# Six of seven Strassen products of a dense layer with channels on partitions: results turned in 32x32 squares

## The chip, the core and the metric

The kernel runs on one core of a Trainium2 chip. The metric is the device time of one execution in microseconds (us), lower is better; the time shown for a kernel is the median of its runs. The core's engines are named as in the profile: PE (TensorE, matrix products; PEld are its weight loads), DVE (VectorE), ACT (ScalarE), POOL (GpSimd) and SP (SyncE). SP, ACT and POOL each also issue DMA transfers, and each runs its own instructions in the order in which they were written.

## What is computed

A transformer block on 2048 tokens with 512 channels, float32. The second half is what matters here: a dense layer to 1792 channels, the Mish activation, and a dense layer back to 512, scaled by `gb` and added to the residual.

```python
x = x + ga * _A_ref(h, A_wqkv, A_wo)             # linear attention
h = _layernorm(x, axis=-1) * (1 + cb) + sb
h = jnp.einsum("bsd,df->bsf", h, w1) + b1        # 512 -> 1792
act = h * jnp.tanh(softplus(h))                  # Mish
x = x + gb * jnp.einsum("bsf,fd->bsd", act, w2)  # 1792 -> 512
```

## The kernel before, in words

Tokens come in four blocks of 512 (b = 0 to 3), channels in tiles of 128, so the hidden layer has 14 tiles (f), taken as 7 pairs (g). Every float32 product is made of three matmuls on upper and lower parts of its operands (`mm3`: upper x upper, upper x lower, lower x upper; its second argument is the stationary operand, the third the moving one). `split` makes these parts: the upper on ACT (line 84), the lower on DVE (line 90).

Blocks 2 and 3 are handled together with a seven-product (Strassen) scheme, for both dense layers. This change is about the second layer of these two blocks, after the helper `two_pairs`/`pair_unit` has made the hidden layer. Its operands are cut in two ways each: tokens in block 2 and block 3, hidden tiles in the even and the odd one of a pair, output channels in a left and a right half of 256. The seven products `m1` to `m7` each run over the 7 pairs. `seventh` makes one product's share of one pair, called a unit here: before, for each of four groups of 128 tokens, an `mm3` with the activations (128 x 128) stationary and the weights (128 x 256) moving, so 12 matmuls of 256 columns; a PSUM bank then holds two groups of 128 tokens by 256 channels. `m1` and `m2` (`e_unit`) are made in the gaps between the products of the first layer (`gap`, called by `pair_unit`); the units of the last pair, and `m4`, `m6`, `m7`, `m5` follow in a loop over `units`, and `m3` ends the kernel, token group by token group. The inner loop of `m3` is no part of this change.

The left operands are sums of the activations of both blocks (`left_sums`, line 1353, DVE) which are then split; in the closing loop `ahead_of` lists these splits, taken from five units ahead on. The weights of a unit come by a DMA that POOL issues (`load_wt`). The residual rows of blocks 2 and 3 (`x1d`, written by `o_post` to DRAM) are loaded by SP (`load_r`) into tiles `rq[n, c, i]`: block, half of the channels, half of the rows or channels. When a product is complete, `finish` adds its two banks where they belong: straight to the residual tiles (`add_r`) or to the running sum `U`, and SP stores finished tiles (`store`). After `m3`, four adds (line 1477) and four stores end the kernel.

The order on each engine is the order of writing, shaped by generators: `spawn` adds one, each `tick()` advances every running generator by a step, and `spawn_idle` adds background work of which `width[0]` (here 3) generators advance per tick. All SBUF tiles `sb(...)` share 101 slots; PSUM has 4 banks under the tag `acc`, 3 under `h` and 1 under `tp`. For blocks that the first layer reads with channels on partitions, `load_squares` loads DRAM rows in 32 x 32 squares (four transfers of 32 partitions for a tile), and `dve.transpose` turns each square in place (line 262).

Of the kernel before, what the change touches and what calls it, by code (L numbers as in the profile page):

```python
# [27 lines left out]
def block_kernel(ctx: ExitStack, tc: tile.TileContext, x, wqkv, wo, w1, b1t, w2, c, wmodt, out):  # L28
    nc = tc.nc
    act, dve, pool, pe, sp = nc.scalar, nc.vector, nc.gpsimd, nc.tensor, nc.sync  # L30
# [4 lines left out]
    drp = ctx.enter_context(tc.tile_pool(name="drp", bufs=1, space=bass.MemoryType.DRAM))  # L35
# [16 lines left out]
    def spawn(gen):  # L52
        fresh.append(iter(gen))

    def spawn_idle(gen):

        idle_work.append(gen)

    def tick():

        running.extend(fresh)
        fresh.clear()
        for g in list(running):
# [10 lines left out]
    def mm3(o, st, mv, start, stop):  # L74

        pe.matmul(o, st[0], mv[0], start=start, stop=False)  # L76
        pe.matmul(o, st[0], mv[1], start=False, stop=False)  # L77
        pe.matmul(o, st[1], mv[0], start=False, stop=stop)  # L78
# [163 lines left out]
    nd, yd = {}, {}  # L242

    def to_dram(key, b, t, v):
        if (key, b) not in nd:
            nd[key, b] = drp.tile([512, D], F32, name=f"{key}d_{b}")
        pool.dma_start(nd[key, b][P * t:P * (t + 1), :], v)

    def load_squares(key, b, order=(0, 2, 1, 3)):


        for j in order:
            y = yd[key, b, j] = sb(f"y_{key}_{b}_{j}")
            for c in range(4):
                lo = P * j + 32 * c
                sp.dma_start(y[32 * c:32 * (c + 1), :].rearrange("q (m r) -> q m r", r=32),
                             nd[key, b][:, lo:lo + 32].rearrange("(m q) r -> q m r", q=32))

    def turn(key, b, j, keep, name, sc0, sh0):

# [299 lines left out]
    for k in range(4):  # L560
        hi, lo = sb(f"hT_x_0_{k}h", F32R), sb(f"hT_x_0_{k}l", F32R)
# [265 lines left out]
    for b in range(1, NB):  # L827
        last = b == NB - 1
# [86 lines left out]
    x1d = {}  # L915

    def o_post(p, b, t):
        r = xt["r", b, t]
        dve.tensor_tensor(r, p, r, op=ALU.add)  # L919
        if b >= 2:  # L920
            yield
            if t % 2 == 0:
                x1d[b, t // 2] = drp.tile([P, 2, D], F32, name=f"x1d_{b}_{t // 2}")
            pool.dma_start(x1d[b, t // 2][:, t % 2, :], r)  # L924

    def o_unit(b, t, tag="acc"):
        p = ps(tag, f"o_{b}_{t}")
# [150 lines left out]
    for b in range(1, NB):  # L1078
        for t in range(4):
            n = 4 * b + t  # L1080
# [161 lines left out]
    G = NF // 2  # L1242
# [70 lines left out]
    L = NB - 2  # L1313
    pairs, EARLY = [5, 6, 0, 1, 2, 3, 4], 5
    banks, rq, U = {}, {}, {}
    width[0] = 3

    def load_r(n, c):

        for i in range(2):  # L1320
            rq[n, c, i] = sb(f"rq_{n}_{c}_{i}", F32, (P, 2, D // 2))
            sp.dma_start(rq[n, c, i], x1d[L + n, i][:, :, D // 2 * c:D // 2 * (c + 1)])

    def store(n, c, i, lo=0, hi=2):
        r0 = 512 * (L + n) + 2 * P * i
        sp.dma_start(out[r0 + P * lo:r0 + P * hi, D // 2 * c:D // 2 * (c + 1)].rearrange("(t p) c -> p t c", p=P),
                     rq[n, c, i][:, lo:hi, :])

    def seventh(name, tag, left, right, n, last):

        if n == 0:
            banks[name] = [ps(tag, f"{name}_{i}") for i in range(2)]
        for t in range(4):
            h = t % 2
            mm3(banks[name][t // 2][:, D // 2 * h:D // 2 * (h + 1)], [a[:, P * t:P * (t + 1)] for a in left], right,
                n == 0 and h == 0, n == last and h == 1)

    def bank(name, i):
        return banks[name][i].rearrange("p (t c) -> p t c", t=2)
# [16 lines left out]
    left, sums_of = {}, {}  # L1356
# [9 lines left out]
    def add_r(n, c, i, v, op=ALU.add):  # L1366
        dve.tensor_tensor(rq[n, c, i], rq[n, c, i], v, op=op)

    def finish(name):
        for i in range(2):  # L1370
            p = bank(name, i)
            if name == "m2":
                U[i] = sb(f"U_{i}", F32, (P, 2, D // 2))
                act.activation(U[i], bank("m1", i), AF.Copy)
                add_r(0, 0, i, bank("m1", i))
                add_r(0, 0, i, p)
                store(0, 0, i)
            if name == "m4":
                add_r(1, 0, i, p, ALU.subtract)
            if name == "m6":  # L1380
                dve.tensor_tensor(U[i], U[i], p, op=ALU.add)
                add_r(0, 1, i, U[i])
            if name == "m7":
                dve.tensor_tensor(U[i], U[i], p, op=ALU.add)
                add_r(1, 0, i, U[i])
                store(1, 0, i)
                add_r(1, 1, i, U[i])
            if name == "m5":
                add_r(0, 1, i, p)
                add_r(1, 1, i, p)  # L1390
                store(1, 1, i)
            yield

    wt, SUM = {}, {"m5": 0, "m6": 1, "m7": 2, "m4": 3}
# [15 lines left out]
    for n, g in enumerate(pairs):  # L1410
        if n < 5:
            if n:
                load_rows(n)
            if n:
                load_wb(pairs[n + 1])
        if n == 5:
            load_wb(pairs[6])
            load_r(0, 0)
        if n == 6:
            for m in pairs[:5]:  # L1420
                load_wt("m4", m)
        def gap(c, m):
            def unit():
                e_unit(c, m)
            return unit

        if n in (3, 5):
            spawn_idle(w2_sums(SUMS_KEPT[n // 2 - 1]))
        if n == 0:
            spawn_idle(w2_sums(2))  # L1430
            begun = [pair_begin(L, pairs[i], ("tp" if i else "h", "acc")) for i in range(2)]
            tick()
        elif n == 1:
            two_pairs(L, pairs[0], g, begun, (gap(0, 0), gap(0, 1)))
            for i in range(2):
                spawn_idle(left_trail(pairs[i]))
        else:
            pair_unit(L, g, n % 2, (gap(1, 0), gap(1, 1)) if n == 2 else (gap(0, n - 1), gap(1, n - 1)))
            if n < EARLY:
                spawn_idle(left_trail(g))  # L1440

    names = ["m4", "m6", "m7", "m5", "m3"]
    units = [(name, n) for name in names for n in range(G)]
    ahead_of = units[EARLY:]
    loads = list(units)
    loads = loads[5:]
    load_r(1, 0)
    tags = {"m4": "h", "m6": "acc", "m7": "acc", "m5": "h"}
    for k, (name, n) in enumerate(units[:4 * G]):
        for _ in range(2 if k in (6, 10, 14, 18) else 1):  # L1450
            if ahead_of:
                nm, m = ahead_of.pop(0)
                spawn(left_prep(nm, pairs[m]))
        for _ in range(2 if k < 3 else 1):
            if loads:
                nm, m = loads.pop(0)
                load_wt(nm, pairs[m])
        if k in (3, 8):
            load_r(k // 8, 1)
        seventh(name, tags[name], left.pop((name, pairs[n])), wt.pop((name, pairs[n])), n, G - 1)  # L1460
        if n == G - 1:
            spawn(finish(name))
        tick()
        if k == 1:
            e_unit(0, G - 1)
            e_unit(1, G - 1)
            spawn(finish("m2"))
            tick()

    last = [ps("acc", f"m3_{t}") for t in range(4)]  # L1470
    for t in range(4):
        p = last[t][:, 0:D // 2]
        for n, g in enumerate(pairs):
            mm3(p, [a[:, P * t:P * (t + 1)] for a in left["m3", g]], wt["m3", g], n == 0, n == G - 1)
        tick()
        v = rq[0, 1, t // 2][:, t % 2, :]
        dve.tensor_tensor(v, v, p, op=ALU.add)
        store(0, 1, t // 2, t % 2, t % 2 + 1)


# [30 lines left out]
```

## Time and profile before

| | before |
|---|---|
| time, median of 3 runs | 488.17 us (488.06 to 488.59) |
| time of the profiled execution | 488.34 us |
| its span, first to last instruction | 486.6 us |
| granted PE clock over the span | 1.000 of full speed |
| PE busy, matmuls | 481.6 us (99%), 2594 of them |
| PEld busy | 406.5 us (84%) |
| DVE / ACT / POOL busy | 378.3 / 295.7 / 148.7 us |
| DMA | 100.66 MB in 91296 packets |

The profiled execution took 1.7 us more than its span; the rest lies around it. In the rows of the profile, an operation is named by its output and inputs, with buffer numbers left out, so that all of `m1` to `m7` are called `m`, and the split left operands `l_m`. Where rows are listed in time, the first two numbers are start and duration in us.

### The profile page before, as it was taken

To read this page: it belongs to the slowest core of one execution; us is meant where nothing else is said; L and a number is where in the kernel's file an instruction comes from. 1 tells how busy PE (TensorE), PEld (TensorE's weight loads), DVE (VectorE), ACT (ScalarE), POOL (GpSimd) and SP (SyncE) were. 2 spreads that over 40 slices of the span, in tenths; PEclk is the share of its full clock that TensorE was granted. 3 is DMA by queue.
4 is the path that set the end of the run, shared out by engine and by line. 5 is a ranking of instruction groups with operands and counts; after the bars stand their busy time and mean duration, and the time that the engine had idled before them with its cause. 6 is when DMAs were issued, how large, how long until landed. Compare 5 with 4: busy or idle time off the path is not lost.

```text
span 486.6 us, 7712 instructions
## 1 busy us (share of the span) xinstructions
PE 481.6 (99%) x2594; PEld 406.5 (84%) x2594; DVE 378.3 (78%) x731; ACT 295.7 (61%) x528; POOL 148.7 (31%) x248
## 2 busy tenths in 40 slices
PE   8999999999999999999999999999999999999997
PEld 6788887878878888888888888888888888899997
DVE  7989988999799699976867665899543666769772
ACT  6777686866546979647767665674165554568100
POOL 4583320000122124103422435225444410545200
PEclk9999999999999999999999999999999999999999
DMA  8805598244863417488799999979999813789412
GB/s 315 292 14 126 143 156 256 68 145 140 294 169 109 133 36 253 131 291 292 250 339 361 335 207 210 347 225 311 373 356 340 238 26 105 193 205 248 114 44 86
DMA packets 91296, 100.66 MB, mean 207 GB/s; under 512 B 32337, under 2 KB 56921, under 8 KB 91258
## 3 DMA queue, kind: packets, MB, share of 16 engines
q1 hardware_dynamic: 62088, 54.68, 35.9%
q0 software_dynamic: 29024, 45.24, 33.5%
q8 instruction: 20, 0.33, 0.3%
q10 hardware_dynamic: 146, 0.26, 0.1%
q14 instruction: 18, 0.15, 0.1%
HBM read 63.97 MB, written 34.08 MB: 201 GB/s over the span
## 4 chain that ended last, share of the span: by engine, by line
PE 93%; DVE 4%; ACT 1%; issue 1%; POOL 0%; ACTq 0%; DVEq 0%
PE p_a L1137 20%; PE p_s L1137 8%; PE oacc L77 5%; PE oacc L78 5%; PE oacc L76 5%; PE m L78 5%; PE m L77 5%; PE m L76 5%; PE o L76 3%; PE o L78 3%; PE o L77 3%; PE pq_a L404 3%; PE pk L78 2%; PE pk L76 2%; PE pk L77 2%; PE gacc L77 2%
## 5 line engine op out<-in xcount | busy, mean ns | idle before, releaser
L207 POOL TENSOR_TENSOR rs_n<-rs_n,half 128x1 f32<-128x1 f32 x16 | 11.4, 712 | 62.2 <-DVE rs_n L202 35.5
L1142 DVE TENSOR_TENSOR cb<-p_s,u 128x512 f32<-128x512 f32 x28 | 19.2, 687 | 13.1 <-ACT u L1178 13.1
L1172 ACT ACTIVATE u<-p_a 128x512 f32<-128x512 f32 x12 | 7.2, 598 | 28.0 <-PE p_a L1137 28.0
L1147 ACT ACTIVATE u<-p_a 128x512 f32<-128x512 f32 x14 | 8.4, 598 | 25.7 <-PE p_a L1137 17.4
L1129 ACT ACTIVATE ub<-cb,b1c 128x512 f32<-128x512 f32 x28 | 20.0, 717 | 4.9 <-DVE cb L1142 4.7
L1408 POOL DMA_DIRECT2D wt_m<-w2t x20 | 14.0, 703 | 27.1 <-DVE cb L1142 14.7
L1178 ACT ACTIVATE u<-p_a 128x512 f32<-128x512 f32 x14 | 8.4, 597 | 15.9 <-PE p_a L1137 15.9
L1142 DVE TENSOR_TENSOR c<-p_a,u 128x512 f32<-128x512 f32 x14 | 9.6, 688 | 9.1 <-PE p_a L1137 7.9
L895 POOL DMA_DIRECT2D rden_d<-rden x2 | 1.4, 720 | 46.3 <-DVE rden L893 46.3
L295 ACT ACTIVATE e_k<-pk 128x512 f32<-128x512 f32 x15 | 8.9, 592 | 10.8 <-PE pk L78 10.8
L774 POOL DMA_DIRECT2D w2b<-w2d x20 | 10.6, 542 | 14.4 <-DMA y_n<-nd 4.8
L768 POOL DMA_DIRECT2D wb<-w2d x14 | 9.9, 711 | 14.9 <-PE p_a L1137 12.4
L1106 ACT ACTIVATE u<-p_a,b1c 128x512 f32<-128x512 f32 x14 | 9.6, 686 | 6.7 <-PE p_a L1137 6.7
L298 DVE SCALAR_TENSOR_TENSOR ku<-e_k,relu_k 128x512 f32<-128x512 f32 x15 | 10.7, 712 | 3.1 <-ACT relu_k L296 3.1
L298 DVE SCALAR_TENSOR_TENSOR q<-e_q,relu_q 128x512 f32<-128x512 f32 x16 | 10.7, 684 | 2.9 <-ACT relu_q L296 2.9
L207 POOL TENSOR_TENSOR rs_x<-rs_x,half 128x1 f32<-128x1 f32 (+1 forms) x10 | 7.8, 782 | 15.8 <-DVE rs_x L202 14.6
L821 POOL DMA_DIRECT2D a1b<-rd_a x10 | 5.4, 542 | 22.4 <-PE p_a L1137 11.4
L307 POOL DMA_DIRECT2D ku<-ku x8 | 7.2, 898 | 16.5 <-DVE ku L298 16.5
L919 DVE TENSOR_TENSOR r<-o,r 128x512 f32<-128x512 f32 x16 | 10.8, 675 | 0.9 <-PE o L78 0.9
L907 DVE SCALAR_TENSOR_TENSOR q<-q,rd 128x512 f32<-128x512 f32 x16 | 10.5, 683 | 0.6 <-DMA rd<-rden_d 0.4
L924 POOL DMA_DIRECT2D x1d<-r x8 | 4.4, 549 | 20.9 <-DVE r L919 20.9
L183 DVE SCALAR_TENSOR_TENSOR wm<-wm,sc_row 128x512 f32<-128x512 f32 x16 | 10.5, 674 | 0.0
(1623 smaller groups left out, 1975.9 us busy)
## 6 DMA issues: line engine op xcount, KB each, us to landing
wm<-in_wmodt_dram SPq DMA_DIRECT2D x24, 256.0 KB, 5.3
w2b<-w2d POOLq DMA_DIRECT2D x20, 256.0 KB, 6.6
wt_m<-w2t POOLq DMA_DIRECT2D x20, 256.0 KB, 4.2
r<-in_x_dram SPq DMA_DIRECT2D x16, 256.0 KB, 3.3
x<-in_x_dram SPq DMA_DIRECT2D x15, 256.0 KB, 4.8
w1p<-in_w_dram SPq DMA_DIRECT2D x14, 256.0 KB, 4.1
w2r<-in_w_dram SPq DMA_DIRECT2D x14, 256.0 KB, 4.8
wb<-w2d POOLq DMA_DIRECT2D x14, 256.0 KB, 4.8
```

Source lines behind the costliest of these rows:

```text
L76: pe.matmul(o, st[0], mv[0], start=start, stop=False)
L77: pe.matmul(o, st[0], mv[1], start=False, stop=False)
L78: pe.matmul(o, st[1], mv[0], start=False, stop=stop)
L207: pool.tensor_tensor(y, y, half[:, lo:hi], op=ALU.pow)
L298: dve.scalar_tensor_tensor(dst, e, 1.0, r, op0=ALU.min, op1=ALU.add)
L404: pe.matmul(p, l, r, start=onto is None and c == 0 and i == 0, stop=c == 1 and i == 2, skip_group_check=onto is not None)
L774: pool.dma_start(w2s[f][i], w2d[f // 2, i][:, f % 2, :])
L919: dve.tensor_tensor(r, p, r, op=ALU.add)
L1129: act.activation(u, p, AF.Mish, bias=b1c[:, f:f + 1])
L1137: pe.matmul(p, st, mv, start=onto is None and c == 0 and i == 0, stop=c == 1 and i == 2, skip_group_check=onto is not None)
L1142: dve.tensor_tensor(out, p, u, op=ALU.add)
L1408: pool.dma_start(v, w2t[g][:, :, SUM[name], :])
```

## The change

The six products other than `m3` swap their operands: the weights (128 x 128 of them, for each half i of the 256 channels) are stationary and the activations of 512 tokens move. A unit is then 6 matmuls of 512 columns, and a PSUM bank holds 128 channels by 512 tokens. The results are combined in that form (`U`, `Q0` for `m1 + m2`, `W1` for `U` less `m4`) and turned back in 32 x 32 squares by `dve.transpose` (`turned`) before they meet the residual tiles, which are loaded and stored in squares too. `m5` and `m7` change places. What `m3` is added to goes to DRAM in squares (`sd`, issued by ACT) and comes back as rows (`rows01`, issued by SP). The turning of `Q0` and `W1` is put off (`settle`, spawned at units 25 and 17 of the closing loop). The stores of block 2's left and block 3's right half go to ACT's queue, those of block 3's left half to SP's. The splits of `m6` for the first four pairs are made earlier, as background work at the last pair. The final four adds come after all generators have run out.

```diff
+    def squares(y, d, col):
+        for c in range(4):
+            lo = col + 32 * c
+            yield (y[32 * c:32 * (c + 1), :].rearrange("q (m r) -> q m r", r=32),
+                   d[:, lo:lo + 32].rearrange("(m q) r -> q m r", q=32))
...
     def load_r(n, c):
         for i in range(2):
-            rq[n, c, i] = sb(f"rq_{n}_{c}_{i}", F32, (P, 2, D // 2))
-            sp.dma_start(rq[n, c, i], x1d[L + n, i][:, :, D // 2 * c:D // 2 * (c + 1)])
+            rq[n, c, i] = sb(f"rq_{n}_{c}_{i}")
+            for sq, rows_ in squares(rq[n, c, i], x1d[L + n], D // 2 * c + P * i):
+                sp.dma_start(sq, rows_)
...
+    def store(n, c, i, eng):
+        for sq, rows_ in squares(rq[n, c, i], out[512 * (L + n):512 * (L + n + 1), :], D // 2 * c + P * i):
+            eng.dma_start(rows_, sq)
 
     def seventh(name, tag, left, right, n, last):
         if n == 0:
             banks[name] = [ps(tag, f"{name}_{i}") for i in range(2)]
-        for t in range(4):
-            h = t % 2
-            mm3(banks[name][t // 2][:, D // 2 * h:D // 2 * (h + 1)], [a[:, P * t:P * (t + 1)] for a in left], right,
-                n == 0 and h == 0, n == last and h == 1)
+        for i in range(2):
+            mm3(banks[name][i], [w[:, P * i:P * (i + 1)] for w in right], left, n == 0, n == last)
...
     def finish(name):
         for i in range(2):
-            p = bank(name, i)
+            p = banks[name][i]
             if name == "m2":
-                U[i] = sb(f"U_{i}", F32, (P, 2, D // 2))
-                act.activation(U[i], bank("m1", i), AF.Copy)
-                add_r(0, 0, i, bank("m1", i))
-                add_r(0, 0, i, p)
-                store(0, 0, i)
-            if name == "m4":
-                add_r(1, 0, i, p, ALU.subtract)
+                U[i], Q0[i] = sb(f"U_{i}"), sb(f"Q0_{i}")
+                act.activation(U[i], banks["m1"][i], AF.Copy)
+                dve.tensor_tensor(Q0[i], p, U[i], op=ALU.add)
             if name == "m6":
-                dve.tensor_tensor(U[i], U[i], p, op=ALU.add)
-                add_r(0, 1, i, U[i])
+                W1[i] = sb(f"W1_{i}")
+                dve.tensor_tensor(U[i], p, U[i], op=ALU.add)
+                dve.tensor_tensor(W1[i], U[i], banks["m4"][i], op=ALU.subtract)
+            if name == "m5":
+                dve.tensor_tensor(U[i], p, U[i], op=ALU.add)
+                t = turned("T5", i, U[i])
+                add_r(0, 1, i, t)
+                if i == 0:
+                    sd[0] = drp.tile([512, D // 2], F32, name="sd")
+                for sq, rows_ in squares(rq[0, 1, i], sd[0], P * i):
+                    act.dma_start(rows_, sq)
+                add_r(1, 1, i, t)
             if name == "m7":
-                dve.tensor_tensor(U[i], U[i], p, op=ALU.add)
-                add_r(1, 0, i, U[i])
-                store(1, 0, i)
-                add_r(1, 1, i, U[i])
-            if name == "m5":
-                add_r(0, 1, i, p)
-                add_r(1, 1, i, p)
-                store(1, 1, i)
+                t = turned("T7", i, p)
+                add_r(1, 0, i, t)
+                store(1, 0, i, sp)
+                add_r(1, 1, i, t)
+                store(1, 1, i, act)
+            yield
+
+    def settle(v, n):
+        for i in range(2):
+            add_r(n, 0, i, turned(f"S{n}", i, v[i]))
+            if n == 0:
+                store(0, 0, i, act)
             yield
...
         if n == 6:
+            for m in pairs[:4]:
+                early_m6.append(left_prep("m6", m))
+                spawn_idle(early_m6[-1])
...
-    names = ["m4", "m6", "m7", "m5", "m3"]
+    names = ["m4", "m6", "m5", "m7", "m3"]
...
-    tags = {"m4": "h", "m6": "acc", "m7": "acc", "m5": "h"}
+    tags = {"m4": "h", "m6": "acc", "m5": "acc", "m7": "h"}
...
-        if k in (3, 8):
-            load_r(k // 8, 1)
+        if k in (11, 14, 17, 20):
+            load_r(*{11: (1, 0), 14: (0, 1), 17: (1, 1), 20: (0, 0)}[k])
+        if k == 25:
+            spawn(settle(Q0, 0))
+        if k == 26:
+            rows01 = [sb(f"rows_{i}", F32, (P, 2, D // 2)) for i in range(2)]
+            for i in range(2):
+                sp.dma_start(rows01[i], sd[0][2 * P * i:2 * P * (i + 1), :].rearrange("(t p) c -> p t c", p=P))
+        if k == 17:
+            spawn(settle(W1, 1))
...
-        v = rq[0, 1, t // 2][:, t % 2, :]
-        dve.tensor_tensor(v, v, p, op=ALU.add)
-        store(0, 1, t // 2, t % 2, t % 2 + 1)
+
+    for _ in range(4):
+        tick()
+    for t in range(4):
+        v = rows01[t // 2][:, t % 2, :]
+        dve.tensor_tensor(v, v, last[t][:, 0:D // 2], op=ALU.add)
+        sp.dma_start(out[512 * L + P * t:512 * L + P * (t + 1), D // 2:D], v)
```

More of the change, by code (lines that the diff above doesn't have):

```diff
@@ L253, in load_squares @@
             y = yd[key, b, j] = sb(f"y_{key}_{b}_{j}")
[L254 to L257, printed above, removed]
+            for sq, rows_ in squares(y, nd[key, b], P * j):
+                sp.dma_start(sq, rows_)
     def turn(key, b, j, keep, name, sc0, sh0):
@@ L921, in o_post @@
             yield
-            if t % 2 == 0:
-                x1d[b, t // 2] = drp.tile([P, 2, D], F32, name=f"x1d_{b}_{t // 2}")
-            pool.dma_start(x1d[b, t // 2][:, t % 2, :], r)
+            if t == 0:
+                x1d[b] = drp.tile([512, D], F32, name=f"x1d_{b}")
+            pool.dma_start(x1d[b][P * t:P * (t + 1), :], r)
     def o_unit(b, t, tag="acc"):
@@ L1320, in load_r @@
         for i in range(2):
-            rq[n, c, i] = sb(f"rq_{n}_{c}_{i}", F32, (P, 2, D // 2))
-            sp.dma_start(rq[n, c, i], x1d[L + n, i][:, :, D // 2 * c:D // 2 * (c + 1)])
[L1324 to L1327, printed above, removed]
+            rq[n, c, i] = sb(f"rq_{n}_{c}_{i}")
+            for sq, rows_ in squares(rq[n, c, i], x1d[L + n], D // 2 * c + P * i):
+                sp.dma_start(sq, rows_)
+    def store(n, c, i, eng):
+        for sq, rows_ in squares(rq[n, c, i], out[512 * (L + n):512 * (L + n + 1), :], D // 2 * c + P * i):
+            eng.dma_start(rows_, sq)
     def seventh(name, tag, left, right, n, last):
@@ L1332, in seventh @@
             banks[name] = [ps(tag, f"{name}_{i}") for i in range(2)]
-        for t in range(4):
-            h = t % 2
-            mm3(banks[name][t // 2][:, D // 2 * h:D // 2 * (h + 1)], [a[:, P * t:P * (t + 1)] for a in left], right,
-                n == 0 and h == 0, n == last and h == 1)
-    def bank(name, i):
-        return banks[name][i].rearrange("p (t c) -> p t c", t=2)
+        for i in range(2):
+            mm3(banks[name][i], [w[:, P * i:P * (i + 1)] for w in right], left, n == 0, n == last)
     def e_unit(c, n):
@@ L1354, in left_sums @@
         sums_of[g] = {"m5": a22, "m7": a21, "m6": a11, "m3": a12}
-    left, sums_of = {}, {}
+    left, sums_of, early_m6 = {}, {}, []
     def left_trail(g):
@@ L1364, in left_prep, with turned, add_r @@
         return left_sums(g) if name == "m4" else split(f"l_{name}_{g}", sums_of[g][name], left, (name, g))
-    def add_r(n, c, i, v, op=ALU.add):
-        dve.tensor_tensor(rq[n, c, i], rq[n, c, i], v, op=op)
+    Q0, W1, sd = {}, {}, {}
+    def turned(name, i, v):
+        t = sb(f"{name}_{i}")
+        dve.transpose(t, v)
+        return t
+    def add_r(n, c, i, v):
+        dve.tensor_tensor(rq[n, c, i], rq[n, c, i], v, op=ALU.add)
     def finish(name):
         for i in range(2):
-            p = bank(name, i)
+            p = banks[name][i]
@@ L1417, in block_kernel @@
             load_wb(pairs[6])
-            load_r(0, 0)
         if n == 6:
+            for m in pairs[:4]:
+                early_m6.append(left_prep("m6", m))
+                spawn_idle(early_m6[-1])
             for m in pairs[:5]:
@@ L1440, in block_kernel @@
                 spawn_idle(left_trail(g))
-    names = ["m4", "m6", "m7", "m5", "m3"]
+    names = ["m4", "m6", "m5", "m7", "m3"]
     units = [(name, n) for name in names for n in range(G)]
-    ahead_of = units[EARLY:]
+    ahead_of = [u for u in units[EARLY:] if u not in units[G:G + 4]]
     loads = list(units)
     loads = loads[5:]
-    load_r(1, 0)
-    tags = {"m4": "h", "m6": "acc", "m7": "acc", "m5": "h"}
+    tags = {"m4": "h", "m6": "acc", "m5": "acc", "m7": "h"}
     for k, (name, n) in enumerate(units[:4 * G]):
```

## The prediction

> **What bounds the kernel now.** The page comes first: busy time by engine, then the chain that ended last.
>
> ```profile
> PE 481.6 (99%) x2594; PEld 406.5 (84%) x2594; DVE 378.3 (78%) x731; ACT 295.7 (61%) x528; POOL 148.7 (31%) x248
> PE 93%; DVE 4%; ACT 1%; issue 1%; POOL 0%; ACTq 0%; DVEq 0%
> ```
>
> PE is the bound: 93% of the chain. A microsecond off PE comes off the time, as long as the others keep up. So I read PE stage by stage, in the busy time of stretches: a second-layer stretch of 512-column matmuls (block 1, 26 of them), one unit of `m1` and the 512-column product behind it, then the nine units up to `m6`, the 21 units of `m6`, `m7`, `m5`, and `m3`. Columns: stretch, its length, then each engine's busy time.
>
> ```profile
> 339.79:345.68 5.89, 5.89 (x27) 4.88 (x26) 4.11 (x9) 0.00 (x0) 5.04 (x10) 1.00 1.36 349
> 360.66:362.10 1.44, 1.44 (x14) 1.43 (x13) 0.18 (x1) 1.19 (x2) 1.44 (x4) 1.00 0.85 282
> 362.10:363.48 1.38, 1.38 (x8) 1.13 (x7) 1.11 (x2) 0.00 (x0) 1.38 (x4) 1.00 0.96 272
> 429.99:442.94 12.95, 12.95 (x109) 12.95 (x108) 10.96 (x17) 8.72 (x17) 4.70 (x7) 1.00 0.74 181
> 442.94:473.31 30.37, 30.37 (x254) 30.28 (x253) 24.73 (x41) 9.12 (x18) 7.45 (x14) 1.00 0.48 132
> 473.31:483.38 10.07, 10.07 (x86) 10.04 (x84) 3.23 (x7) 0.00 (x0) 0.00 (x0) 1.00 0.27 91
> ```
>
> A 512-column matmul takes 5.89 / 26 = 0.2265 us, a 256-column one 1.44 / 12 = 0.120: twice the latter costs 0.0135 more for the same columns. PEld is busy all the time where 256 columns move and 83% where 512 do. The clock column is 1.00 throughout. DVE is the engine next to full (24.73 of 30.37).
>
> **PE, part by part.** A unit falls from 1.44 to 6 x 0.2265 = 1.359 us. Twelve units lie in gaps of the first layer; there the product behind a unit takes 1.38 instead of 1.36 as well, so 12 x (0.081 + 0.02) = 1.2. The nine units to `m6`: 12.95 - 9 x 1.359 = 0.72. The 21 after it: 30.37 - 21 x 1.359 = 1.83, in which one stall lies: `m6`'s first lower part came late.
>
> ```profile
> 442.49 0.68 DVE L90 TENSOR_TENSOR l_m_5l<-u,l_m_5h 128x512 fp32r<-128x512 f32 x1
> 443.23 0.38 PE L78 MATMUL m<-wt_m,l_m_5l 128*128 128x256 f32 x1
> 443.45 0.28 PE L76 MATMUL m<-wt_m,l_m_5h 128*128 128x256 f32 x1
> ```
>
> The changed kernel makes four of `m6`'s splits earlier, at the last pair, where DVE and ACT have room: 4 x 0.6 of DVE against idle times of 1.31 and 2.29 before these two rows (without that cover, up to 2.4 us late).
>
> ```profile
> 425.10 0.69 DVE L90 TENSOR_TENSOR a_8l<-u,a_8h 128x512 fp32r<-128x512 f32 x1 [1.31 <-ACT a_8h L84]
> 430.22 0.69 DVE L90 TENSOR_TENSOR a_9l<-u,a_9h 128x512 fp32r<-128x512 f32 x1 [2.29 <-ACT a_9h L84]
> ```
>
> PE together: 1.2 + 0.72 + 1.83 = 3.75, taken as 3.8. `m3` stays at 10.07. The loads of `m5`/`m7` weights by POOL wait for slots that come free no later than before, and residual loads are all issued before `m5` ends; both at nothing. The bounds are 3.5 (no gain behind units, the stall stays) and 3.9.
>
> The rule that speaks against this gain: the Trainium skill, "TensorE: Matmul & The Clock Gate", section "Wait — 56ns, not 53.3ns?", puts the fixed cost per warm matmul at 2.5 ns, by which (an estimate from that page) the 42 units would save about 0.6 us; the rows above differ, 13.5 ns per matmul, and decide.
>
> **DVE, ACT and SP after `m5`.** Here the change adds work. Per product, in DVE operations of 128 x 512: `m2` 4 becomes 2, `m4` 2 becomes 0, `m6` 4 stays, `m5` 4 becomes 8, `m7` 6 stays, `settle` adds 8: 20 become 28. The first stretch loses six, the end gains. Their prices: 0.60 apart when independent, 0.72 when one needs the one before, a turn about 0.70.
>
> ```profile
> 452.64 0.69 DVE L1381 TENSOR_TENSOR U<-U,m 128x512 f32<-128x512 f32 x1 [1.04 <-PE m L78]
> 453.36 0.69 DVE L1367 TENSOR_TENSOR rq<-rq,U 128x512 f32<-128x512 f32 x1
> 453.97 0.68 DVE L90 TENSOR_TENSOR l_m_4l<-ub,l_m_4h 128x512 fp32r<-128x512 f32 x1
> L262 DVE STREAM_TRANSPOSE hf_n<-y_n x8: 668/703/708, 300.9 to 312.4; 128x512 f32<-128x512 f32 x8
> 472.80 2.48 DVE L1367 TENSOR_TENSOR rq<-rq,m 128x512 f32<-128x512 f32 x4 [2.53 <-PE m L78]
> 483.59 0.42 DVE L1477 TENSOR_TENSOR rq<-rq,m 128x256 f32<-128x256 f32 x1 [2.10 <-PE m L78]
> 484.04 0.33 SPq L1326 DMA_DIRECT2D out_dram<-rq x1
> ```
>
> I walk the built order of the changed kernel by hand, with 0 where PE ends `m5`. PE ends `m7` at 7 x 1.36 = 9.5 and `m3` at 19.6. Between `m6` and `m5` DVE has 17 operations, 10.7 us in 9.5, so it starts on `m5` at 0.8. First `sd` tile ready at 2.9, second at 6.2. ACT issues its four transfers at about 0.5 each until 8.3; queued behind them on ACT is the last split of `m3` (upper part to 8.9), and DVE's lower part waits for that until 9.6. PE wants it at 9.5 + 6 x 0.36 = 11.7: no stall, 2 us to spare. Then DVE turns and adds `Q0` (10.9 and 12.2), and `m7`, waiting since 9.5, is added at 13.5 and 14.1 for its first half, 15.4 and 16.1 for its second. The final adds of groups 0 and 1 follow from the queue; those of 2 and 3 are again set by PE. So DVE is 3 us behind and catches up before the end, at no cost to PE.
>
> The cost is in the stores: 24 transfers of 64 KB in runs of 128 bytes, 16 on ACT's queue and 8 on SP's, issued from 10.9 on, where before two stores of 256 KB were left. In the built program the transfers of SP and ACT share eight completion semaphores, and an issue waits until the transfer before it on its semaphore has landed. Such waits show already, if short:
>
> ```profile
> SPq L101 <- DMA x<-in_x_dram: 1.3, 4, 0.3
> ```
>
> No row shows a store in squares; the nearest is the load in squares (same sizes and runs, the other way), 16 of them undisturbed: minimum, median, maximum of issue in ns, then of landing in us, then one microsecond there, whose last two columns are the DMA share and GB/s. Below them the other square loads, made beside other traffic, and the issues of the four row stores that end the kernel now, with their size and median landing.
>
> ```profile
> L256 SPq DMA_DIRECT2D y_n<-nd x16: 326/487/773, 277.9 to 285.8; - x16
> DMA to landing us min/median/max: 2.1/2.2/2.6
> 280.00:281.00 1.00, 1.00 (x6) 0.84 (x5) 1.00 (x2) 1.00 (x3) 0.00 (x0) 1.00 0.85 131
> ```
>
> ```profile
> L256 SPq DMA_DIRECT2D y_x<-xd x16: 333/487/919, 62.2 to 71.1; - x16
> DMA to landing us min/median/max: 2.0/3.3/5.3
> ```
>
> ```profile
> out_dram<-rq SPq DMA_DIRECT2D x4, 128.0 KB, 1.7
> ```
>
> Call the landing L. SP issues `m7`'s first tile from 13.6 (four, the last at 15.1); the last of its second tile waits for that one, so it goes at 15.1 + L or, bound by issue, 17.1. ACT's last tile starts when this has landed, by the shared semaphore, and needs three more issues (1.5) and a landing: the end is max(17.1, 15.1 + L) + 2L + 1.5. The last row store lands at 19.6 + 0.66 (PE's end to issue, the rows at 483.38 and 484.04) + 1.7 = 21.9, as before. So the tail costs: L = 1.8 (near the 1.7 of a row store) 0.3; L = 2.2, 1.3; L = 2.6, 2.5; L = 3.3, 4.6 us. I take 2.2, since the sizes and runs are those of that row and PE's stage has hardly other traffic. Sum against the profiled execution: 488.34 - 3.8 + 1.3 = 485.8. The median of the runs is 0.17 below that execution, so **485.7 us**.
>
> **Rivals.**
> 1. Tail hidden: stores land like row stores, 1.8 or less. For it: nothing has to be fetched from DRAM. Against: 512 runs per transfer and two queues at once. 488.17 - 3.8 + 0.2 = 484.6.
> 2. Contended landing: two queues put out twice the 128-byte rate of the load row, whose DMA share is already 0.85, so L is 3.3, the other row. Tail 4.6: 489.0, no change. The tail eats the gain of 3.8 at L = 3.0.
> 3. Slower: small writes cost the DMA engines twice what small reads do. A load transfer takes 64 KB / 131 GB/s x 0.85 = 0.42 us of all 16; 24 stores at 0.84 are 20 us from 11.6 on, ending at 32 instead of 22: 488.17 - 3.8 + 10 = 494.4. It decides from about 0.58 us per transfer. Against it: row stores occupy no more than loads of their size. The Trainium skill, "DMA: Bandwidth & Descriptors", section "Specifications", says that below 512 B the engines do read-modify-write, which would be such a mechanism; no run shown so far has a store that small.
> 4. The change does not do what it says: 512 columns with these operands run no faster per column, PE gives 0.6 or less, the tail stays: 488.8. Against: the block-1 row has the same form.
>
> **How the numbers follow.** Forecast 0.48 (its own range, L from 2.0 to 2.6: 485.1 to 486.9), rival 1 0.19, rival 2 0.15, rival 3 0.13, rival 4 0.05. About 0.2% (1 us) is what a measurement of this kernel tells from no change. Faster by more: the forecast and rival 1, 0.67; within: 0.10 of rival 2 and 0.04 of rival 4, 0.14; slower: rival 3 and the rest of rivals 2 and 4, 0.19. The range reaches from rival 1's near end, 484.1, past rival 2, to 489.4, and leaves out rival 3 and a few hundredths at either end.
>
> **What would show it.** Right: unit pitch 1.36 in all 42 units, 252 matmuls fewer, `m3` starting 3.8 us earlier and still 10.1 long, no PE gap there; DVE idle before the last two final adds; the span ending some 1.3 us later after PE's end than the 3.2 of now (486.6 - 483.38), with ACT's square stores last to land at about 2.2 each. Wrong: a PE gap near `m3`'s seventh pair (ACT behind `sd`), square stores landing at 3 or more, or the DMA share in the last 10 us at its ceiling.

## The result, and the profile after

| | before | after |
|---|---|---|
| time, median of 7 runs each, same chip | 488.59 us (488.05 to 488.92) | 490.15 us (489.64 to 490.71) |
| span of the profiled execution | 486.6 us | 488.2 us |
| PE busy, matmuls | 481.6 us, 2594 | 478.3 us, 2342 |

The change makes the kernel slower: the ratio after to before is 1.0037, with a 95% interval of 1.0025 to 1.0048. The forecast was 485.7 us with a range of 484.1 to 489.4, so both the sign and the range missed.

The busy time of the changed kernel first, then the stretches that answer to those of before: one unit, the nine units up to `m6`, the 21 units of `m6`, `m5`, `m7`, and `m3` (stretch, its length, busy time of PE, PEld, DVE, ACT, POOL; the last three columns are PE clock, DMA share and GB/s).

```profile
PE 478.3 (98%) x2342; PEld 393.4 (81%) x2342; DVE 383.9 (79%) x739; ACT 295.7 (61%) x528; POOL 148.8 (30%) x248
```

```profile
360.85:362.21 1.36, 1.36 (x8) 1.13 (x6) 0.10 (x1) 1.20 (x2) 1.36 (x4) 1.00 0.94 271
429.06:441.30 12.24, 12.24 (x56) 10.13 (x55) 10.46 (x17) 6.83 (x13) 4.39 (x7) 1.00 1.34 218
441.30:469.87 28.57, 28.57 (x128) 23.66 (x127) 23.68 (x38) 9.16 (x18) 7.82 (x15) 1.00 1.12 149
469.87:479.95 10.08, 10.08 (x85) 10.01 (x83) 7.68 (x14) 0.00 (x0) 0.00 (x0) 1.00 0.81 149
```

PE does what was forecast. A unit takes 1.36 us, the nine take 12.24 (12.95 before), the 21 take 28.57 (30.37), `m3` 10.08, all without a gap; this is the mechanism that the prediction had. PE ends at 479.95, where it ended at 483.38: 3.43 us are won. But the span ends 8.25 us after that (488.2 - 479.95), where it was 3.2. The 5.0 us of longer tail eat the gain and 1.6 more.

The tail, in order of time. First DVE (start, duration, operation), from the last turns on:

```profile
474.56 0.71 DVE L1370 STREAM_TRANSPOSE T<-m 128x512 f32<-128x512 f32 x1
475.31 1.29 DVE L1374 TENSOR_TENSOR rq<-rq,T 128x512 f32<-128x512 f32 x2
476.52 0.75 DVE L1510 TENSOR_TENSOR rows<-rows,m 128x256 f32<-128x256 f32 x2
477.61 0.42 DVE L1510 TENSOR_TENSOR rows<-rows,m 128x256 f32<-128x256 f32 x1 [0.34 <-PE m L78]
480.12 0.42 DVE L1510 TENSOR_TENSOR rows<-rows,m 128x256 f32<-128x256 f32 x1 [2.09 <-PE m L78]
```

DVE waits only for PE before its last two adds: it is not late. Then the issues of SP from 479.5 to 483.7, and those of ACT in the same stretch (the first row of each begins just before it):

```profile
478.41 1.95 SPq L1332 DMA_DIRECT2D out_dram<-rq  x2
480.46 2.55 SPq L1511 DMA_DIRECT2D out_dram<-rows  x4
```

```profile
478.31 5.60 ACTq L1332 DMA_DIRECT2D out_dram<-rq  x3
```

Three of the four final adds are done by 478.1, but SP issues the row stores only from 480.46, when its last square store is out, and needs 2.55 us for the four. ACT makes three issues in 5.60 us. The third, the first of its last tile, stands still for 3.3 us of these, from 480.27 to 483.59. By the semaphore events of the trace it waits for SP's last square store, whose completion semaphore it shares and which lands at 483.23, 3.5 us after this issue:

```profile
479.69 0.67 SPq L1332 DMA_DIRECT2D out_dram<-rq  x1
```

ACT's last store then goes at 485.05 and lands at 487.05. The issues of all square stores by queue (number, then minimum, median, maximum in ns, first and last start):

```profile
L1332 ACTq DMA_DIRECT2D out_dram<-rq x16: 322/510/1242, 471.4 to 485.1; - x16
L1332 SPq DMA_DIRECT2D out_dram<-rq x8: 339/736/1239, 474.1 to 479.7; - x8
```

Of these, the ones from 473.2 to 479, with their landings in us, and the stretch in which both queues are at work:

```profile
L1332 ACTq DMA_DIRECT2D out_dram<-rq x8: 322/720/1242, 472.9 to 478.3; - x8
L1332 SPq DMA_DIRECT2D out_dram<-rq x7: 339/804/1239, 474.1 to 478.4; - x7
DMA to landing us min/median/max: 3.0/3.2/3.7
```

```profile
473.00:479.00 6.00, 6.00 (x53) 6.00 (x52) 4.62 (x9) 0.00 (x0) 0.00 (x0) 1.00 0.92 137
```

The same kind of store, alone on ACT's queue a few microseconds earlier (`sd`), and one microsecond of that:

```profile
L1396 ACTq DMA_DIRECT2D sd<-rq x8: 309/509/566, 463.3 to 468.0; - x8
DMA to landing us min/median/max: 1.8/2.0/2.0
```

```profile
465.00:466.00 1.00, 1.00 (x6) 0.81 (x5) 0.93 (x3) 0.00 (x0) 0.00 (x0) 1.00 0.77 116
```

One queue moves 116 GB/s at a DMA share of 0.77, two together 137 at 0.92. So a transfer takes 64 KB / 116 x 0.77 = 0.43 us of all engines in the one case and 65.5 / 137 x 0.92 = 0.44 in the other. By these two rows the second queue adds 18% of throughput. What it also adds is waiting: issues of 0.51 become 0.72 to 0.80, landings of 2.0 become 3.2. That the engines are full is a reading and not shown by the share alone: it sums the times of packets, and it stands at 1.34 and 1.12 in two of the stretches above. The Trainium skill, "DMA: Bandwidth & Descriptors", section "Issuing engines are not separate DMA queues", says that transfers of several issuing engines interleave on the same 16 DMA engines and that issuing from more of them saves only issue time; these rows agree.

### The profile page after: what moved, and what is told of

It is laid out like the page before. It is cut to its first block, busy times and chain, and to the rows that moved or that the text cites. A ratio compares the mean times of both kernels' runs of the same rounds, so it can differ in the third digit from the quotient of the medians.

```text
span 488.2 us, 7282 instructions
## 1 busy us (share of the span) xinstructions
PE 478.3 (98%) x2342; PEld 393.4 (81%) x2342; DVE 383.9 (79%) x739; ACT 295.7 (61%) x528; POOL 148.8 (30%) x248
## 4 chain that ended last, share of the span: by engine, by line
PE 92%; DVE 4%; ACT 1%; issue 1%; POOL 0%; ACTq 0%; DVEq 0%
PE p_a L1142 20%; PE p_s L1142 8%; PE oacc L76 5%; PE oacc L77 5%; PE oacc L78 5%; PE m L76 5%; PE m L78 5%; PE m L77 5%; PE o L76 3%; PE o L78 3%; PE o L77 3%; PE pq_a L409 3%; PE pk L76 2%; PE pk L78 2%; PE pk L77 2%; PE gacc L77 2%
## 5 line engine op out<-in xcount | busy, mean ns | idle before, releaser
L84 ACT ACTIVATE l_m_4h<-u 128x512 fp32r<-128x512 f32 x2 | 1.3, 633 | 22.2 <-DMA sd<-rq 18.8
```

## Experiments

My theory A was that the late square stores fill the DMA engines. The rivals were a late DVE or ACT (B, H), the waits on shared semaphores by themselves (D), and the order in the queues (E, and F, which joins queue order and semaphores); G, I and J are named where they come up. Ratios are to the kernel before, on the same chip, with a 95% interval.

| kernel | median, us | ratio |
|---|---|---|
| changed kernel | 490.15 | 1.0037 (1.0025 to 1.0048) |
| no late square stores | 485.28 | 0.9928 (0.9915 to 0.9941) |
| late stores in 1 KB runs, 24 issues | 487.01 | 0.9970 (0.9958 to 0.9982) |
| late stores in 1 KB runs, 6 issues | 485.32 | 0.9933 (0.9920 to 0.9945) |
| all 24 squares on one queue | 492.56 | 1.0082 (1.0069 to 1.0095) |
| row stores on POOL | 489.96 | 1.0026 (1.0016 to 1.0035) |
| `sd` stores on SP | 489.56 | 1.0019 (1.0008 to 1.0030) |
| Q0 early (on ACT) | 490.03 | 1.0037 (1.0023 to 1.0051) |
| Q0 early, all of `m7` on ACT | 490.83 | 1.0054 (1.0038 to 1.0070) |
| Q0 early and `sd`, both on SP | 487.73 | 0.9980 (0.9972 to 0.9989) |
| the same, row stores on POOL | 488.01 | 0.9987 (0.9979 to 0.9996) |
| the same, `sd` read by POOL | 486.92 | 0.9963 (0.9948 to 0.9977) |
| the same, `m7`'s left half stored by POOL | 487.35 | 0.9975 (0.9965 to 0.9985) |
| `m7` in rows | 497.96 | 1.0192 (1.0175 to 1.0208) |
| `m7` in rows, POOL helping | 498.69 | 1.0211 (1.0194 to 1.0228) |

**What the stores cost.** All late square stores left out:

```diff
     def store(n, c, i, eng):
-        for sq, rows_ in squares(...):
-            eng.dma_start(rows_, sq)
+        pass
```

> The changed kernel without its 24 late square stores: three quarters of the result's last two blocks are not written, all work of PE, DVE and the sd round trip stays. Gives PE's gain and DVE's walk without the tail. Theory F: tail after DVE's last add 3.0 us as in the kernel before, time 3.5 to 3.8 us under it: 484.5 to 485.1. If the tail had another cause (the row stores' order, DVE late), 486 or more.

Measured: 485.28 us, 3.46 us under the kernel before on the same chip (488.74), just short of the expected 3.5 to 3.8. The last add is at 480.23 (480.12 in the changed kernel), the span ends at 483.5, and the row stores are quick again:

```profile
L1510 SPq DMA_DIRECT2D out_dram<-rows x4: 332/344/424, 477.1 to 480.7; - x4
DMA to landing us min/median/max: 1.7/1.7/1.7
```

So all work of PE and DVE stands and is worth 0.72% (3.5 us); the 24 stores cost 1.0037 - 0.9928 = 1.09%, or 5.3 us.

**Which property of them.** The same stores in long runs:

```diff
-        for sq, rows_ in squares(...):
-            eng.dma_start(rows_, sq)
+        for q in range(4):
+            r0 = 512 * (L + n) + 2 * P * i + 64 * q
+            eng.dma_start(out[r0:r0 + 64, D // 2 * c:D // 2 * (c + 1)].rearrange("(q t) r -> q t r", t=2),
+                          rq[n, c, i][32 * q:32 * (q + 1), :].rearrange("q (t r) -> q t r", t=2))
```

> The 24 late stores keep their number, size (64 KB), queues, order and semaphores, but each writes 64 half rows of 1 KB instead of 512 pieces of 128 bytes; the result then lies in other places, so its values are not the reference's. Theory A (the late square stores fill the DMA engines: each takes about 0.43 us of all 16, and two queues offer 4 per us): the tail after PE's end falls from 8.2 to some 3.5 us, time 485.0 to 486.0, landings under 2.5 us. Rival B (DVE and ACT come late after m5, so that the stores start late): nothing changes, 489.5 or more. Rival D (the waits on shared completion semaphores between SP and ACT, whatever the length of a piece): the waits stay, most of the tail stays, 488 or more.

```profile
L1333 ACTq DMA_DIRECT2D out_dram<-rq x16: 577/606/702, 471.4 to 481.8; - x16
L1333 SPq DMA_DIRECT2D out_dram<-rq x8: 570/604/776, 474.1 to 479.0; - x8
DMA to landing us min/median/max: 2.1/2.1/2.4
```

```profile
476.00:480.00 4.00, 4.00 (x35) 3.93 (x33) 1.74 (x5) 0.00 (x0) 0.00 (x0) 1.00 0.88 201
```

Number, order, queues and semaphores are the same, and 0.67% (3.3 us) of the 5.3 is gone. Landings are back at 2.1, a transfer takes 65.5 / 201 x 0.88 = 0.29 us of the engines, and ACT's long halt has vanished with the late landing that it waited for. This speaks against B and D as causes by themselves. But the time is 1 us above what I expected: A isn't all. The rest was split by storing each tile at once, in the same long runs:

```diff
+        r0 = 512 * (L + n) + 2 * P * i
+        eng.dma_start(out[r0:r0 + 2 * P, D // 2 * c:D // 2 * (c + 1)].rearrange("(t p) r -> p t r", p=P),
+                      rq[n, c, i].rearrange("p (t r) -> p t r", t=2))
```

> The changed kernel with the six late tiles stored in 1 KB runs, one store of 256 KB for each tile instead of four of 64 KB: 6 issues instead of 24, the same bytes; the result lies in other places, so its values are not the reference's. If the number of issues in front of the row stores was the rest of the tail: as without late stores, 485.2 to 485.8. If the bytes are: as with long runs in 24 issues, 486.7 to 487.2.

```profile
475.00:479.00 4.00, 4.00 (x36) 4.00 (x35) 2.40 (x6) 0.00 (x0) 0.00 (x0) 1.00 0.92 305
```

485.32 us: as without late stores. The 1.5 MB stored in this way cost no time that shows. The 1.8 us (0.37%) from 24 stores of 32 partitions to 6 of 128 partitions are issues and shape together, which this run does not part: at about the same DMA share the engines now move 305 GB/s (row stores among them) instead of 201. The Trainium skill, "DMA: Bandwidth & Descriptors", section "Rules for kernel authors", advises one transfer over 128 partitions in place of two over disjoint halves of them; the two runs, with quarters, point the same way.

**One queue.**

```diff
-                store(1, 0, i, sp)
+                store(1, 0, i, act)
```

> All 24 late square stores on ACT's queue, SP keeps only the four row stores. Theory A (the engines are the limit, 0.43 us per transfer, and one queue at 0.5 us per issue nearly fills them): the second queue bought nothing. 24 issues x 0.5 from 471.4 end at 483.5, landing 2.0 to 2.2 until SP's row stores join: time 488 to 489, faster than the changed kernel by 1 to 2 us. Rival E (two queues do put out more than one, and the order of the stores is at fault): ACT has 8 more issues to make, so later by 2 to 4 us, 492 to 494.

```profile
L1332 ACTq DMA_DIRECT2D out_dram<-rq x24: 322/501/539, 472.8 to 489.2; - x24
DMA to landing us min/median/max: 1.8/2.0/2.7
```

```profile
476.97 3.55 ACTq L1332 DMA_DIRECT2D out_dram<-rq  x2
```

Here both are wrong in part. The time lies in Rival E's range, and A's 488 to 489 is missed by 4 us. But issues and landings are those of an undisturbed queue (0.50 and 2.0), as A says: contention of the two queues makes 3.2 out of 2.0, and one queue alone moves 118 GB/s (from 486 to 489 us), close to the 137 of two. The time is 2.4 us longer than the changed kernel's because 24 issues take 16.9 us, 0.70 each instead of 0.50, for ACT halts: two issues take 3.55 us in the second fence, since a square store waits there on a semaphore that SP's first row store holds until 480.1. With Q0 early, the same step gave 490.83 against 490.03:

> Q0 early as in the run before last, and the 16 stores of m7 all on ACT's queue. Theory A: 16 x 0.5 from 474.1 end at 482.2, land at 484.4: 487.0, that is no better than with two queues by more than 0.5, and landings near 2.0 until the row stores come. Rival E: 1.5 us or more slower than Q0 early on two queues.

The difference is less than Rival E's 1.5 us, and the intervals overlap. Theory A's 487.0 is missed by 3.8 us; what holds up the kernel with Q0 early is told further down.

**Queue order, semaphores and the late DVE.** The row stores on POOL, whose transfers share no semaphore with SP's and ACT's (`pool.dma_start` for `sp.dma_start` in the last line):

> The four row stores that end the kernel go out on POOL's queue instead of SP's; POOL's transfers share no completion semaphore with SP's and ACT's. Theory F (row stores queued behind SP's stretched square stores, and ACT's last tile waiting 3.3 us on a shared semaphore until the first row store has landed): ACT's last tile goes at about 480.3 instead of 483.6, time 487.5 to 488.7. Rival A alone (the DMA engines are simply full until 483 to 484): 489.5 to 490. Rival G (POOL's stores are slower to land, 4 us and more): 490 or more, with these four landing last.

```profile
L1511 POOL DMA_DIRECT2D out_dram<-rows x4: 540/546/552, 477.0 to 480.6; - x4
DMA to landing us min/median/max: 4.1/4.5/5.4
...
L1332 ACTq DMA_DIRECT2D out_dram<-rq x16: 322/509/1398, 471.1 to 485.0; - x16
L1332 SPq DMA_DIRECT2D out_dram<-rq x8: 341/817/1774, 473.8 to 479.8; - x8
DMA to landing us min/median/max: 2.4/3.0/5.8
```

They go out when ready, at 477.0 to 480.6, 2 to 4 us earlier than on SP, but take 4.5 us to land beside the square stores (2.5 in the changed kernel), so most of the head start is lost. And ACT's last square store still goes at 485.0, now held up by semaphores of SP's square stores. 489.96 is A's number; F's 487.5 to 488.7 was wrong. G's landings of 4 us and more came as well, though ACT's square stores, not these four, are the last to land; the time alone doesn't tell A from G. Nor does it help much to free DVE, by issuing the `sd` stores on SP in place of ACT:

> The eight square stores to sd go out on SP's queue instead of ACT's, so that ACT's last split of m3 isn't queued behind them. Theory F: DVE's wait of 2.17 us before l_m_4l goes, Q0's and m7's turns and all 24 late square stores come 2.2 us earlier, and with them the row stores that wait in SP's queue: about 2 us faster than the changed kernel, 487.8 to 488.5. Rival H (the lateness of DVE is without effect, since PE and the DMA engines set the end): 489.5 to 490.2.

DVE's wait of 2.17 us is gone, and ACT's square stores start at 469.2 instead of 471.4. But 489.56 us is Rival H's number: by the ratios the time falls by only 0.2% (0.9 us), and the intervals overlap. SP then held `m7`'s stores behind `sd`'s rows (the first goes at 474.7, not earlier than the 474.1 of the changed kernel).

**Fewer stores at the end.** Q0's residual loaded, and Q0 turned and stored, 12 units earlier:

```diff
-        if k in (11, 14, 17, 20):
-            load_r(*{11: (1, 0), 14: (0, 1), 17: (1, 1), 20: (0, 0)}[k])
-        if k == 25:
+        if k in (8, 11, 14, 17):
+            load_r(*{8: (0, 0), 11: (1, 0), 14: (0, 1), 17: (1, 1)}[k])
+        if k == 13:
             spawn(settle(Q0, 0))
```

> Q0's residual is loaded at unit 8 and Q0 turned, added and stored at unit 13 instead of 20 and 25, so that 8 of the 24 square stores leave the last 17 us; nothing else changes. Theory A: 8 x 0.43 = 3.4 us of engine work leave the tail, 486 to 487.5. Rival B (late DVE and ACT): DVE reaches m7's turns 2.7 us earlier, but the end is set by the row stores after PE, so at most 1 us, 489. Rival D (shared semaphores): ACT's last tile no longer waits for a row store, 487 as well; it is told from A by the landings, which stay at 3 or more by D's reading and fall to 2 to 2.6 by A's. Risk: DVE is 81% busy at units 7 to 20, and a late left part would show as a gap on PE.

```profile
448.81 7.49 ACTq L1332 DMA_DIRECT2D out_dram<-rq  x8
456.35 0.63 ACT L84 ACTIVATE l_m_2h<-ub 128x512 fp32r<-128x512 f32 x1 [11.67 <-DMA rq<-x1d]
```

```profile
PE m L76 <- ACT l_m_4h L84: 1.0, 1, 1.0
PE m L78 <- DVE l_m_4l L90: 0.2, 1, 0.2
```

No gain, 490.03, against A's 486 to 487.5. The tail after the last add is shorter (487.3 - 481.45 = 5.8 us against 488.2 - 480.12 = 8.1), but ACT's queue stood for 7.49 us with Q0's stores. The splits behind them were late, with them DVE's part and the `sd` stores (from 466.7, not 463.3), and PE waited 1.2 us for `m3`'s last split, which ACT makes behind `sd`. The landings, by which A and D were to be told apart, stayed at 3.5 to 4.1 us: D's sign, not A's. Moved to SP, with the `sd` stores, and all residuals loaded earlier:

```diff
+        if k in (8, 10, 12, 14):
+            load_r(*{8: (0, 0), 10: (1, 0), 12: (0, 1), 14: (1, 1)}[k])
+        if k == 16:
             spawn(settle(Q0, 0))
...
-                store(0, 0, i, act)
+                store(0, 0, i, sp)
...
-                    act.dma_start(rows_, sq)
+                    sp.dma_start(rows_, sq)
```

> The sd stores on SP, and Q0's residual loaded at unit 8, the other residuals at 10, 12, 14, Q0 turned and stored at unit 16 on SP's queue, where ACT's splits don't wait behind its issues. Theory F: 16 square stores are left after m7, the first at about 470.7, SP is through with its eight before the second row store is ready, and the tail after the last add of DVE is 3 to 4 us as in the kernel before: 485.0 to 486.3. Rival I (issues on SP delay the residual loads, or the new order delays a left part): a gap on PE, 487 or more.

487.73: faster than both, 1.4 us short of Theory F's range. The number lies in Rival I's, but the gap on PE that Rival I rests on isn't there. Adding POOL for the row stores changed nothing beyond the intervals (488.01):

> As the run before with the four row stores on POOL's queue. Theory F: SP's queue is empty by then, so within 0.5 us of the run before. If shared semaphores still hold ACT's last tile there, 1 us or more faster than it.

Adding POOL for the loads of `sd`'s rows instead:

> As the kernel with Q0 early and sd stored by SP, with the two loads of sd's rows on POOL's queue: there SP's queue stood behind them until the last sd store had landed (m7's first square store on SP at 474.0 instead of 471.2), and ACT's fourth square store waited 3 us on a semaphore that such a load held. Theory F: m7's 16 stores go from 471.2 on, take the engines 16 x 0.43 = 6.9 us, land by 480, and the row stores find both queues free: tail after DVE's last add 3.0 to 3.5 us, 485.0 to 485.8, 2 to 2.7 us faster than that kernel. Rival A alone (full engines, no queue and no semaphore matters): no gain over it, 487.4 to 488.

```profile
472.89 1.29 DVE L1374 TENSOR_TENSOR rq<-rq,T 128x512 f32<-128x512 f32 x2
478.64 0.75 DVE L1510 TENSOR_TENSOR rows<-rows,m 128x256 f32<-128x256 f32 x2 [4.46 <-DMA rows<-sd]
480.06 0.75 DVE L1510 TENSOR_TENSOR rows<-rows,m 128x256 f32<-128x256 f32 x2 [0.66 <-DMA rows<-sd]
```

486.92 us is the lowest median of the versions that compute the whole result, 0.37% under the kernel before (interval 0.23% to 0.52%); the interval overlaps with that of Q0 early and `sd`, both on SP, and with that of the next run. The expected 485.0 to 485.8 wasn't reached: read beside `m7`'s square stores, `sd`'s rows land after 5.3 to 6.0 us, and the final adds wait for them, no longer for PE. With `m7`'s left half stored by POOL and `sd`'s rows back on SP:

> The kernel with Q0 early and sd stored and read back by SP, with the eight square stores of m7's left half on POOL's queue, so that SP's queue holds nothing between sd's rows and the row stores. If the row stores' place behind SP's squares was what was left of its tail: the row stores go at 477 to 480.7, 485.3 to 486.5. If the engines, full with squares, hold them up wherever they are queued: 487 to 488, with row stores landing at 3 us and more.

487.35, in the second of the expected ranges. SP issues its row stores from 477 on, but the second takes 1.06 us to issue and 5.1 to land. On SP's queue as on POOL's, the row stores are held up beside the square stores.

**No square store after `m7`.** `m7` was left as before, with results in rows, and the three parts that `m7` and `m3` are added to went through DRAM earlier:

```diff
+        if name == "m7":
+            for t in range(4):
+                h = t % 2
+                mm3(banks[name][t // 2][:, D // 2 * h:D // 2 * (h + 1)], [a[:, P * t:P * (t + 1)] for a in left],
+                    right, n == 0 and h == 0, n == last and h == 1)
+            return
...
+        if k == 23:
+            load_rows_sd(1, 0)
...
+            load_rows_sd(1, 1)
+            load_rows_sd(0, 1)
```

> m7 is left as in the kernel before (256 channels moving, results in rows), so five of the seven products are swapped, and the three parts that m7 or m3 are added to go back through DRAM before: written in squares by SP, read in rows by POOL. After m7 only whole rows are stored, and Q0's eight squares by ACT. PE gives back 7 x 0.081 = 0.6 us. Theory A with F (what the late square stores cost is their time on full engines next to the row stores): tail after DVE's last add about 3.3 us, 485.5 to 486.5. Rival J (16 square stores of SP after m5 end too late, and m7's and m3's rows come back after PE is done): DVE waits on the rows at the end, 487.5 or more.

> As the run before with the eight square stores of the lower right part on POOL's queue beside SP's. If one queue's issues (0.5 each) limit the way through DRAM, the rows come 1 to 2 us earlier and the time falls by up to that; if the engines limit it, no change within 0.5 us.

Both are 2% slower, and POOL's help changed nothing beyond the intervals. POOL's issues and DVE's adds of the first of them:

```profile
465.81 1.44 POOL L1431 DMA_DIRECT2D rows<-sd  x2 [14.34 <-DMA rq<-x1d]
467.25 3.23 POOL L1445 DMA_DIRECT2D wt_m<-w2d  x6
484.69 2.85 POOL L1431 DMA_DIRECT2D rows<-sd  x4 [14.21 <-DMA out_dram<-rq]
```

```profile
487.95 1.88 DVE L1405 TENSOR_TENSOR rows<-rows,m 128x512 f32<-128x512 f32 x3 [14.43 <-DMA rows<-sd]
```

Rival J's mechanism, and far larger than I had thought. POOL's load of the rows stands for 14.21 us, because SP's square stores to `sd` end too late:

```profile
467.54 13.46 SPq L1426 DMA_DIRECT2D sd<-rq  x16
```

By the semaphore events of the trace the last of these 16, issued at 480.06, lands at 484.07, and POOL's wait for it ends at 484.10. (The row above names a store to the result as the releaser: that store uses a semaphore for which the load also waits, and its update is the latest by the profile.) With POOL's help for the stores, the weights of `m3` stood behind them in POOL's queue, and PE waited 7.0 us in all:

```profile
PE m L76 <- DMA wt_m<-w2d: 7.0, 3, 5.0
```

## Why the prediction was wrong, by its own steps

- PE, 3.75 taken as 3.8: the mechanism was right, the size a little too large. The 21 units saved 1.80 (forecast 1.83) and `m6`'s stall is gone, the nine 0.71 (0.72), and the nine start 0.93 us earlier (1.2). In the end 3.43 by the trace, just under the lower bound of 3.5, and 3.5 by the kernel without late stores. The row of this kernel, 13.5 ns per matmul, held against the 2.5 ns of the Trainium skill, "TensorE: Matmul & The Clock Gate", section "Wait — 56ns, not 53.3ns?".
- DVE, ACT and SP after `m5`: right. With 0 = 460.34, DVE starts on `m5` at 0.8, ACT is free of `sd` at 8.2 (8.3), and SP's first `m7` store goes at 13.7 (13.6). The adds end at 14.3 and 16.3 (14.1 and 16.1). No gap on PE. (By its own list of operations the first stretch loses four on DVE, not six; no term rests on it.)
- The tail's **L = 2.2** is the step that failed: the tail was to cost 1.3 us and cost 5.0. L was taken from a row in which one queue worked alone. Where two work, L is 3.2 at the median, up to 3.7. The first term of the formula had the same error: it let SP issue at 0.5 each, so that the last square goes at 17.1; issues of 0.74 at the median and up to 1.24 made it 19.3 (479.7). The wait was right: ACT's halt ended with the landing of SP's last square, as assumed. The formula with L = 3.3 gives max(17.1, 18.4) + 6.6 + 1.5 = 26.5, a tail of 4.6. Measured: the last store, issued at 485.1, lands 2.0 later, 26.7 after 460.34. That these agree so well is in part luck: SP's last square goes 0.9 later than the 18.4 of this sum, and ACT's last store, beside none of SP's by then, lands in 2.0 and not 3.3.
- Engine time alone doesn't give this end either: 24 stores at 0.43 us are 10.3 us, which from the first issue at 471.4 would end at 481.7, and over the last 10 us the DMA share is only 0.73. From there to 487.05 it is the chain of waits, which long landings stretch: SP's last square, ACT's halt for it, the last tile's four issues and one more landing.
- Rival 2 therefore is nearest to what happened; it had 0.15. Its price of 489.0 was 1.2 too low: PE gave 3.4 and not 3.8, the tail took 5.0 and not 4.6, and the kernel before stood at 488.59 beside these runs, not at 488.17. The number that should have raised it stood in the quoted rows: 0.42 us of all engines per transfer, used only for rival 3. 24 of these are 10.1 us, while two queues at 0.5 us per issue offer them in 6 to 8 us. The landing time of a quiet stretch did not hold there.
- Rival 2's wording was not right: two queues did not put out twice the rate of one, but 16 to 18% more (137 GB/s against 118 and 116).
- Rival 1 (tail hidden) was right for the same bytes in long runs and whole tiles only: 485.32.
- Rival 3 (small writes cost the engines twice what small reads do) is refuted: 0.43 to 0.44 us per store against 0.42 per load, both in runs of 128 bytes.
- Rival 4 is refuted by the pitch of 1.36.

Of the signs named beforehand as wrong, one came clearly: square stores landing at 3 or more. The DMA share was 0.92 from 473 to 479, but 0.73 over the last 10 us.

What stays open: how much of the last 1.8 us is the number of issues and how much the shape over 32 partitions, and what shared semaphores cost in the changed kernel by themselves; no run removed these alone. How full the DMA engines were is likewise argued from rates and landings.

## What to carry to other kernels

Price the transfers at a kernel's end in engine time first (number x bytes / GB/s x DMA share, from a row of the same shape), and compare the sum with the time in which the queues would issue them; here that sum was the larger (10 us against 6 to 8), and the landing time from a quiet stretch didn't hold. Then follow the chain of issues, landings and shared semaphores to the last store, with the longer landing in each place. A faster PE was worth nothing here, as its results came out in pieces of 128 bytes at the very end: what helped was to move those stores ahead, onto a queue behind which no compute waits; whole tiles over 128 partitions at the end would cost nothing, but only if the rows are there in time. And follow each queue and each transfer that a moved one waits for: in this case early stores on ACT stopped PE for 1.2 us, and a load on POOL stood 14 us for the square stores whose rows it was to read.

## What the runs showed of the hardware that I had not expected

- Two queues with stores in runs of 128 bytes move 137 GB/s, one moves 116 to 118; the issues themselves get longer, from 0.51 to 0.72 and 0.80 us at the median.
- 1.5 MB in 1 KB runs go at 201 GB/s in stores of 64 KB over 32 partitions and at 305 in stores of 256 KB over 128, at DMA shares of 0.88 and 0.92.
- Beside square stores other transfers land late too: row stores of 128 KB at 2.5 us from SP and 4.5 from POOL, instead of 1.7 from an otherwise empty SP queue, loads of `sd`'s rows at 5.3 to 6.0.
